# Routing tail of an RWKV, top-1 MoE and MLP kernel: tile 11's diagonal products earlier on ScalarE, and scalings, one-hots, slots and low rows of tiles 9 to 11 on GpSimd

## The chip, the cores and the metric

The kernel runs on one core of a Trainium2 chip. The metric is device time in microseconds (us) of one execution, taken as the median of several runs; one further execution was recorded by the hardware profiler. Engine names are those of the profile: PE is TensorE's matmul, PEld its weight load, DVE is VectorE, ACT is ScalarE, POOL is GpSimd, SP is the engine that issues most of the transfers. A q behind a name (SPq, POOLq) means the engine's instruction queue.

## The reference, cut to what matters

```python
def reference(**kwargs):
    attn_out = _attn_ref(...)          # linear attention: state = w*state + k v^T, y = r (state + u k v^T)
    x = attn_out.transpose(0, 2, 1, 3).reshape(1536, 384)
    x = _moe_ref(x, ...)
    return _moe2_ref(x, ...)           # h = x @ w_in; g = h * clip(h + 3, 0, 6) / 6; g @ w_out

def _moe_ref(x, w_gate, w1, w2, capacity):
    logits = x @ w_gate                # 8 experts
    expert_idx = argmax(logits)        # one expert for a token
    gate_w = softmax(logits)[expert_idx]
    for i in range(N):                 # tokens take the expert's places in order, up to capacity
        e = expert_idx[i]
        if counts[e] < capacity:
            disp[e, counts[e]] = x[i]; pos[i] = counts[e]; counts[e] += 1; keep[i] = True
    y = relu(disp @ w1) @ w2           # for each expert
    out[i] = gate_w[i] * y[expert_idx[i], pos[i]] if keep[i] else 0
```

## The kernel before

The kernel has three stages: attention with routing (to about 88 us in the trace), the experts (to about 219 us), and the last MLP. All of its instructions are placed by hand: each engine works through its own list in the order in which the code was written, and a semaphore holds an instruction until what it needs is there. An instruction that waits holds everything behind it on its engine.

Attention works on 12 tiles of 128 tokens, called T or t. For a tile, `bonus(T)` lets ACT write the diagonal products (8 small activations, one for each head, scaled by `dg`) into the tile x; `values` and `carried` are matmuls; `finish_x` adds their sum to x on DVE; `turn` transposes x on PE and ACT copies the result to `xT`; `gate` multiplies it with the gate's weights. Then comes `route(t)`: a list of about a dozen small DVE steps, handed out by `tick`. They find the largest logit, the one-hot of the chosen expert (`oh_all`), the ranks among tokens (`rank_mm`, a few small PE matmuls that `ranks` issues), the softmax scale `sm`, and `sf`, the token's place. `slots` is that place as an integer. Tiles 0 to 7 are routed in groups of four, whose scales are called `gsm`.

The rows of x, multiplied by the scale, go into the table `xs` in DRAM, sorted by expert, by one indirect transfer for each tile (`scale`, then `scatter`, L703; GpSimd issues it). `fetch(e)` reads an expert's first 224 rows back into `xr`. `fetch(0)` comes behind the scatters of tiles 0 to 8. Tiles 9, 10 and 11 reach expert 0 in another way, without the table: `first` is a one-hot of 128 tokens by 224 places, `lasth` the scaled rows rounded to the short format, `lastl` the remainder ("low rows"), and `late_rows(t)` multiplies both by the one-hot on PE into `px` (L684). The rows out of `xr` are added to `px` by transposing matmuls (L879). When `px` is whole, ACT and DVE cast it to `xh` and `xl` (L925 to L929), and the first expert matmul `psm` (L997) starts. Tiles 9 to 11 are scattered all the same, because the other experts need them. These three scatters write the table that `fetch(0)` reads, so the first of them waits until that read has landed.

Weights arrive in pieces of 768 KB, `raw`; ACT rounds a piece to its high part (`wah`, `wbh`) and DVE or GpSimd make the low part (`wal`, `wbl`, L188 and L194). `keep_warm(n)` issues n matmuls on zeros.

Of the kernel before, what the change touches and what calls it, by code (L numbers as in the profile page):

```python
# [8 lines left out]
F32 = mybir.dt.float32  # L9
# [11 lines left out]
P = 128  # L21
# [24 lines left out]
WIN = 224  # L46
# [19 lines left out]
def kernel(  # L66
# [150 lines left out]
        for _ in range(n):  # L217
            begin(lo_eng=lo_eng)

    late, px0, first, last_h, last_l = [], [], {}, {}, {}  # L220
    xr_t = {}
    spreads, places, outs = [], [], []

# [18 lines left out]
    def attention():  # L242
        actx = ExitStack()
        with actx:
# [343 lines left out]
            def route(t):  # L588
                if t < GRP * NGRP:
                    if t % GRP == GRP - 1:  # L590
                        route_group(t - GRP + 1)
                    return
                last, tail = t >= LATE, t == NTILE - 1
                pl = lgt.pop(t)
                l, po = pl[:, 0:E], pl[:, 64:64 + 2 * E]
                rk, pe = pl[:, 192:192 + E], pe_all[:, t, :]
                oh = oh_all[:, t, :]
                oh2 = oh.unsqueeze(1).to_broadcast([P, 2, E])
                slot = slots[:, t:t + 1]
# [12 lines left out]
                def rank_mm():  # L612
                    base_mm(po, t, True, False)
                    nc.tensor.matmul(po, tri, oh2, start=False, stop=True)

                def inverse():
                    V.reciprocal(sm, sm)
                    if last:
                        hi = lastp.tile([P, DM], F32R, name=f"lasth{t}")
                        nc.scalar.activation(hi, x_t[t], AF.Copy, scale=sm)  # L620
                        last_h[t] = hi
                        if t == NTILE - 2:
                            nc.scalar.activation(x_t[t], x_t[t], AF.Copy, scale=sm)
                            lo = lastp.tile([P, DM], F32R, name=f"lastl{t}")
                            nc.gpsimd.tensor_tensor(out=lo, in0=x_t[t], in1=hi.bitcast(F32), op=ALU.subtract)
                            last_l[t] = lo

                def low_rows():
                    o = first[t]
                    if t != NTILE - 2:  # L630
                        lo = lastp.tile([P, DM], F32R, name=f"lastl{t}")
                        V.scalar_tensor_tensor(
                            out=lo, in0=xs_t[t], scalar=sm, in1=last_h[t].bitcast(F32), op0=ALU.mult, op1=ALU.subtract
                        )
                    else:
                        lo = last_l[t]
                    first[t] = ((last_h[t], o), (lo, o))

                def done():
                    if last:  # L640
                        o = lastp.tile([P, WIN], F32R, name=f"first{t}")
                        V.tensor_scalar(
                            out=o, in0=col, scalar1=sf, scalar2=None, op0=ALU.is_equal
                        )
                        first[t] = o
                        xs_t[t] = x_t[t]
                        last_ops[t] = [low_rows]
                    V.tensor_scalar(out=slot, in0=sf, scalar1=float(FAR), scalar2=None, op0=ALU.add)
                    if t == NTILE - 2:
                        ready.append((slot, x_t.pop(t)))  # L650
                    else:
                        scat.append((slot, x_t.pop(t), sm))

                todo.append([
                    lambda: V.tensor_reduce(out=mx, in_=l, axis=AX.X, op=ALU.max),
                    lambda: V.scalar_tensor_tensor(
                        out=rk, in0=l, scalar=mx, in1=rank, op0=ALU.is_equal, op1=ALU.mult
                    ),
                    diff,
                    lambda: V.tensor_reduce(out=m2, in_=rk, axis=AX.X, op=ALU.max),  # L660
                    lambda: V.tensor_tensor(out=oh, in0=rk, in1=m2.to_broadcast([P, E]), op=ALU.is_equal),
                    [0, rank_mm],
                    lambda: V.tensor_reduce(out=sm, in_=gex[:, t % GRP, :], axis=AX.X, op=ALU.add),
                    inverse,
                    lambda: V.tensor_tensor(
                        out=sel, in0=po.rearrange("p (a e) -> p a e", a=2), in1=oh2, op=ALU.mult
                    ),
                    lambda: V.tensor_reduce(out=pe.unsqueeze(2), in_=sel, axis=AX.X, op=ALU.add),
                    lambda: V.tensor_scalar(
                        out=sf, in0=pe[:, 0:1], scalar1=cap_f, scalar2=pe[:, 1:2], op0=ALU.is_lt, op1=ALU.mult  # L670
                    ),
                    done,
                ])

# [72 lines left out]
            for T in range(NTILE - 1):  # L747
# [49 lines left out]
                    scatter()  # L797
                if T == 10:
                    drain(1)
                    scale()  # L800
                    scatter()
                    scatter()
                    scale()
# [29 lines left out]
            load_to(7)  # L833
            T = NTILE - 1
            carried(T)
            bonus(T)
            values(T, 0)
            ranks(0)
            keep_warm(3)
# [1 line left out]
            finish_x(T, 0)  # L841
            drain(0)
            values(T, 1)
            keep_warm(3)
            gate(T - 1)
            finish_x(T, 1)
            load_to(8)
            keep_warm(2, 0)
            route(T - 1)
            tick(3)  # L850
            turn(T)
            tick(2)
            finish(T - 2)
            late_rows(LATE, 0)
            keep_warm(2, 0)
            ranks(0)
            keep_warm(3, 0)
            tick(5)
            gate(T)
            route(T)  # L860
            xr = xr_t.pop(0)
            todo.reverse()
            tick(5)
            late_rows(LATE, 1)
            keep_warm(3, 0)
            ranks(0)
            todo.reverse()
            while len(todo) > 1:
                tick()
            finish(T - 1)  # L870
            tick(2)
            drain(0)
            finish(T)
            scale()
            scatter()
            keep_warm(3, 0)
# [6 lines left out]
            late_rows(LATE + 1)  # L883
            late_rows(T)
            scatter()
            scale(nc.vector)
            scatter()
            late.extend((lambda: rest(nc.vector, slice(HC, PC)), lambda: low(nc.vector)))

# [548 lines left out]
```

## Time and profile before

| what | us |
|---|---|
| median of 3 runs | 428.57 |
| lowest and highest | 428.19, 429.74 |
| the profiled execution's own time | 428.45 |
| its span, first to last instruction | 426.7 |
| PE, DVE, ACT, POOL busy in the span | 414.3, 256.2, 204.1, 177.0 |
| mean granted clock of TensorE | 0.995 |

The span is 1.75 us shorter than the profiled execution's own time; what lies around the span is start and end. PE is busy for 97% of the span, but a busy PE also counts matmuls that wait in its pipeline, so the order of events around the change has to be read from the timeline.

### The profile page before, as it was taken

How to read it: one execution, taken by the hardware profiler on the slowest of the kernel's cores; microseconds unless marked ns; L12 is line 12 of the kernel's file. 1: busy time of each engine (PE TensorE's matmuls, PEld its weight loads, DVE VectorE, ACT ScalarE, POOL GpSimd, SP SyncE). 2: the span in 40 equal slices, each digit the busy share in tenths (PEclk: the TensorE clock that was granted, in tenths of full speed). 3: DMA queues.
4: the chain of work that ended last, by engine and by line, in shares of the span. 5: the costliest groups of instructions: out<-in, count | busy, mean ns of one | idle time of the engine just before them, and what ended most of it. 6: DMA issues, size and time to landing. Idle time of an engine off the chain costs nothing.

```text
span 426.7 us, 8128 instructions
## 1 busy us (share of the span) xinstructions
PE 414.3 (97%) x3165; PEld 401.4 (94%) x3165; DVE 256.2 (60%) x474; ACT 204.1 (48%) x434; POOL 177.0 (41%) x146
## 2 busy tenths in 40 slices
PE   7999999999999999999999999999999999999992
PEld 4789999899999999999999999999999999999992
DVE  6997999797886775886978689661313022130310
ACT  2364569665735746757536263352505134260520
POOL 4875594327667567466000000002625225260441
PEclk9999999999999999999999999999999999999998
DMA  7988999556398898998521610001000000100001
GB/s 215 247 259 261 285 351 386 205 200 270 103 236 282 214 306 241 258 306 237 204 84 65 212 61 28 0 5 52 3 37 20 0 2 0 57 1 2 0 22 44
DMA packets 15953, 61.41 MB, mean 144 GB/s; under 512 B 2912, under 2 KB 4832, under 8 KB 15904
## 3 DMA queue, kind: packets, MB, share of 16 engines
q1 hardware_dynamic: 11808, 53.78, 40.9%
q0 software_dynamic: 1968, 4.73, 3.1%
q10 hardware_dynamic: 2128, 2.27, 1.8%
q8 instruction: 27, 0.44, 0.5%
q14 instruction: 22, 0.18, 0.1%
HBM read 53.30 MB, written 7.48 MB: 142 GB/s over the span
## 4 chain that ended last, share of the span: by engine, by line
PE 71%; DVE 8%; issue 8%; DMA 6%; POOL 4%; ACT 2%; SPq 0%; POOLq 0%; DVEq 0%; ACTq 0%
PE psh L1115 20%; PE pso L1138 20%; PE psm L997 11%; PE pym L1036 6%; DMA raw<-in_w_dram 4%; PE pym L1032 3%; PE py L421 2%; DMA hTt<-in_hT_dram 2%; POOL gl L1104 2%; PE pym L1033 2%; DVE A L400 1%; PE psa L394 1%; DVE rTt L354 1%; PE py L413 1%; PE pl L475 1%
## 5 line engine op out<-in xcount | busy, mean ns | idle before, releaser
L1119 DVE SCALAR_TENSOR_TENSOR g<-g,psh 128x384 f32<-128x384 f32 x64 | 35.4, 553 | 98.8 <-ACT g L1118 98.4
L1118 ACT ACTIVATE g<-psh,three 128x384 f32<-128x384 f32 x64 | 37.4, 584 | 73.3 <-PE psh L1115 73.2
L1104 POOL TENSOR_TENSOR gl<-g,gh 128x384 fp32r<-128x384 f32 x40 | 40.3, 1012 | 51.1 <-ACT gh L1103 51.1
L1156 POOL DMA_INDIRECT out_dram<-o,cid x12 | 11.8, 981 | 116.1 <-ACT o L1154 107.9
L1032 PE MATMUL pym<-h,wbh 128*128 128x448 f32 x120 | 38.4, 378 | 0.1
L194 POOL TENSOR_TENSOR wal<-raw,wah 128x1536 fp32r<-128x1536 f32 x7 | 24.6, 3519 | 24.0 <-ACT wah L188 15.9
L1103 ACT CAST gh<-g 128x384 fp32r<-128x384 f32 x64 | 32.3, 504 | 3.5 <-DVE g L1119 3.5
L1003 ACT ACTIVATE h<-psm 128x448 fp32r<-128x448 f32 x32 | 17.5, 548 | 31.1 <-PE psm L997 29.0
L1115 PE MATMUL psh<-y2l,wbh 128*128 128x384 f32 x96 | 32.4, 337 | 0.0
L1115 PE MATMUL psh<-y2l,wah 128*128 128x384 f32 x96 | 32.4, 337 | 0.0
L1115 PE MATMUL psh<-y2h,wah 128*128 128x384 f32 x96 | 32.3, 336 | 0.0
L1115 PE MATMUL psh<-y2h,wbh 128*128 128x384 f32 x96 | 32.3, 336 | 0.0
L1115 PE MATMUL psh<-y2h,wbl 128*128 128x384 f32 x96 | 32.1, 335 | 0.0
L1115 PE MATMUL psh<-y2h,wal 128*128 128x384 f32 x96 | 32.1, 335 | 0.0
L1138 PE MATMUL pso<-wah,gh 128*128 128x384 f32 x96 | 32.1, 334 | 0.0
L1138 PE MATMUL pso<-wbh,gh 128*128 128x384 f32 x96 | 32.1, 334 | 0.0
L1138 PE MATMUL pso<-wbh,gl 128*128 128x384 f32 x96 | 32.1, 334 | 0.0
L1138 PE MATMUL pso<-wal,gh 128*128 128x384 f32 x96 | 32.1, 334 | 0.0
L1138 PE MATMUL pso<-wah,gl 128*128 128x384 f32 x96 | 32.1, 334 | 0.0
L1138 PE MATMUL pso<-wbl,gh 128*128 128x384 f32 x96 | 32.1, 334 | 0.0
L997 PE MATMUL psm<-xh,wah 128*128 128x224 f32 x192 | 31.9, 275 | 0.1
L997 PE MATMUL psm<-xh,wal 128*128 128x224 f32 x192 | 31.7, 275 | 0.0
(192 smaller groups left out, 1144.0 us busy)
## 6 DMA issues: line engine op xcount, KB each, us to landing
raw<-in_w_dram SPq DMA_DIRECT2D x32, 768.0 KB, 7.9
tokt<-in_tok_dram SPq DMA_DIRECT2D x12, 576.0 KB, 6.2
raw<-in_w_in_dram SPq DMA_DIRECT2D x8, 768.0 KB, 4.8
raw<-in_w_out_dram SPq DMA_DIRECT2D x8, 768.0 KB, 5.0
hTt<-in_hT_dram SPq DMA_DIRECT2D x12, 448.0 KB, 7.3
xs<-zero SPq DMA_DIRECT2D x8, 336.0 KB, 5.3
xr<-xs ACTq DMA_DIRECT2D x6, 336.0 KB, 7.3
xr<-xs SPq DMA_DIRECT2D x2, 336.0 KB, 3.5
```

The source lines that it names most:

```text
L194: eng.tensor_tensor(out=lo[:, sl][:, h], in0=raw[:, h], in1=hi[:, sl][:, h].bitcast(F32), op=ALU.subtract)
L997: nc.tensor.matmul(ps[:, fi, :], wa_tile(a, k, 2 * q + fi), b[:, k, :], start=n == k == 0 and not (both and fi), stop=n == 2 and k == KD - ...
L1003: nc.scalar.activation(hh, ps, AF.Relu)
L1032: nc.tensor.matmul(py[k], w2h[:, w], h2, start=f == 0, stop=False)
L1036: nc.tensor.matmul(py[k // 2][:, k % 2, :], a[:, w], h2[:, i], start=n == 0, stop=n == 3 * NF - 1)
L1103: nc.scalar.copy(gh, g)
L1104: (nc.vector if any(do) else nc.gpsimd).tensor_tensor(out=gl, in0=g, in1=gh.bitcast(F32), op=ALU.subtract)
L1115: nc.tensor.matmul(ps, wa_tile(a, k, f), y, start=n == 0, stop=n == 3 * KD - 1)
L1118: nc.scalar.activation(g, ps, AF.Relu, bias=three)
L1119: nc.vector.scalar_tensor_tensor(out=g, in0=g, scalar=6.0, in1=ps, op0=ALU.min, op1=ALU.mult)
L1138: nc.tensor.matmul(po, a[:, sl], c[:, wo], start=(h == 0 or (b, s) in acc) and f == 0 and n == 0, stop=(h == 1 or defer) and f == NF - 1 a ...
L1156: apart(outs, nc.gpsimd.indirect_dma_start(out=out, out_offset=bass.IndirectOffsetOnAxis(ap=cid[:, t:t + 1], axis=0), in_=o, in_offset=Non ...
```

## The change

ACT's order in iteration T = 10 changes: `bonus(11)` stands ahead of a weight cast of 1536 columns and ahead of one scaling, and the scaling of tile 7 goes to GpSimd. For tiles 9 and 10 the one-hots `first`, the `slots` and the low rows go from DVE to GpSimd; their scaling is on ACT for both. For tile 11 these stay on DVE, and its scaling goes from DVE to GpSimd. The tail's order is written anew: `gate(11)` stands ahead of tile 9's rows, tile 9's scatter ahead of tile 10's one-hot, and the transposes of `xr` behind tile 10's rows. Eight of 19 keep-warm matmuls are gone.

```diff
-                        if t == NTILE - 2:
+                        if not tail:
                             nc.scalar.activation(x_t[t], x_t[t], AF.Copy, scale=sm)
...
+                    if tail:
                         V.scalar_tensor_tensor(
                             out=lo, in0=xs_t[t], scalar=sm, in1=last_h[t].bitcast(F32), op0=ALU.mult, op1=ALU.subtract
                         )
                     else:
-                        lo = last_l[t]
+                        nc.gpsimd.tensor_tensor(out=lo, in0=xs_t[t], in1=last_h[t].bitcast(F32), op=ALU.subtract)
...
+                own = nc.gpsimd if last and not tail else V
+
+                def spots():
+                    o = lastp.tile([P, WIN], F32R, name=f"first{t}")
+                    own.tensor_scalar(
+                        out=o, in0=col, scalar1=sf, scalar2=None, op0=ALU.is_equal
+                    )
...
+                    own.tensor_scalar(out=slot, in0=sf, scalar1=float(FAR), scalar2=None, op0=ALU.add)
+                    if last and not tail:
                         ready.append((slot, x_t.pop(t)))
...
                 if T == 10:
                     drain(1)
-                    scale()
+                    bonus(T + 1)
+                    scale(nc.gpsimd)
                     scatter()
                     scatter()
                     scale()
...
             carried(T)
-            bonus(T)
             values(T, 0)
...
+            gate(T)
+            finish(T - 2)
+            scatter()
+            late_rows(LATE)
+            tick(7)
+            finish(T - 1)
+            scatter()
+            route(T)
             tick(5)
             keep_warm(3, 0)
             ranks(0)
+            late_rows(LATE + 1)
+            tick(6)
+            finish(T)
             drain(0)
+            xr = xr_t.pop(0)
             for n in range(2 * KD):
                 k, c = divmod(n, 2)
                 nc.tensor.matmul(
                     px0[k][:, c * HW:(c + 1) * HW], xr[:HW, c, k * P:(k + 1) * P], ident[:HW, :HW],
...
             late_rows(T)
-            scatter()
-            scale(nc.vector)
+            scale(nc.gpsimd)
             scatter()
```

In the order lists below, `x_757`, `x_834`, `x_917`, `x_1022` and `x_1124` are the tiles x of t = 6, 7, 8, 9 and 10; `x_1255` is that of t = 11 before, and `x_1218` that of t = 11 now. The bracket names the semaphores that an instruction waits for: `DMAHW` those of transfers issued by SP or ACT, `DMASW` those of GpSimd's indirect transfers.

On ACT, in iteration T = 10, this stands before:

```order
L693 ACTIVATE x_757<-x_757,gsm_985 128x384
L693 ACTIVATE x_834<-x_834,gsm_985 128x384
L693 ACTIVATE x_917<-x_917,sm_1098 128x384 [waits DVE_49]
L610 ACTIVATE gex_239<-d_1194 128x8 [waits DVE_49]
L188 CAST wah_1015<-raw_913 128x1536 [waits DMAHW5_49]
L429 ACTIVATE x_1255<-tokt_832,dg_1200 128x48 [waits DMAHW4_49,DMASW2_49]
L429 ACTIVATE x_1255<-tokt_832,dg_1200 128x48 x7
L466 COPY xT_1280<-pt_1276 128x384 [waits PE_49,Activation_49]
```

And this now:

```order
L694 ACTIVATE x_757<-x_757,gsm_985 128x384
L429 ACTIVATE x_1218<-tokt_832,dg_1200 128x48 [waits DMAHW4_49,DMASW2_49,DVE_49]
L429 ACTIVATE x_1218<-tokt_832,dg_1200 128x48 x7
L694 ACTIVATE x_917<-x_917,sm_1098 128x384 [waits DVE_49]
L610 ACTIVATE gex_239<-d_1194 128x8 [waits DVE_49]
L188 CAST wah_1015<-raw_913 128x1536 [waits DMAHW5_49]
L466 COPY xT_1280<-pt_1276 128x384 [waits PE_49,Activation_49]
```

The eight products of tile 11 moved ahead of the cast, and the scaling of tile 7 left ACT.

On GpSimd, from the scatter of tile 6 to the end of the tail, this stands before (tile 10's low rows, then the scatters of tiles 10, 9 and 11):

```order
L703 DMA xs_60<-x_757,slots_76 12288x384 [waits Activation_49]
L703 DMA xs_60<-x_834,slots_76 12288x384 [waits Activation_49]
L703 DMA xs_60<-x_917,slots_76 12288x384 [waits DMASW0_49,DVE_49,Activation_49]
L625 TENSOR_TENSOR lastl10_1354<-x_1124,lasth10_1351 128x384 [waits DVE_49,Activation_49]
L703 DMA xs_60<-x_1124,slots_76 12288x384 [waits DMAHW2_49,DMASW1_49,DVE_49]
L703 DMA xs_60<-x_1022,slots_76 12288x384 [waits DMASW2_49,Activation_49]
L703 DMA xs_60<-x_1255,slots_76 12288x384 [waits DMASW3_49,DVE_49]
```

Now the scaling of tile 7 (`L696 TENSOR_SCALAR x_834<-x_834,gsm_985 128x384`) stands ahead of the scatter of tile 6, and from the scatter of tile 8 on the engine has:

```order
L704 DMA xs_60<-x_917,slots_76 12288x384 [waits DMASW0_49,DVE_49,Activation_49]
L640 TENSOR_SCALAR first9_1291<-col_250,sf_1198 128x224 [waits DVE_49]
L648 TENSOR_SCALAR slots_76<-sf_1198 128x1
L633 TENSOR_TENSOR lastl9_1339<-x_1022,lasth9_1285 128x384 [waits Activation_49]
L704 DMA xs_60<-x_1022,slots_76 12288x384 [waits DMAHW2_49,DMASW1_49,Pool_49]
L640 TENSOR_SCALAR first10_1361<-col_250,sf_1314 128x224 [waits DVE_49]
L648 TENSOR_SCALAR slots_76<-sf_1314 128x1
L633 TENSOR_TENSOR lastl10_1364<-x_1124,lasth10_1355 128x384 [waits Activation_49]
L704 DMA xs_60<-x_1124,slots_76 12288x384 [waits DMASW2_49,Pool_49]
L696 TENSOR_SCALAR x_1218<-x_1218,sm_1372 128x384 [waits DVE_49,PE_49]
L704 DMA xs_60<-x_1218,slots_76 12288x384 [waits DMASW3_49,DVE_49,Pool_49]
```

The first late scatter, which waits for the landing of `fetch(0)` (`DMAHW2_49`), stood behind tile 10's low rows; now tile 10's one-hot, slots and low rows stand behind it.

On PE, from the rank matmul of tile 11 to the first expert matmul, the list now is this (before, the six transposes of `xr` stood ahead of tile 10's rows):

```order
L614 MATMUL pl_1335<-oh_all_65,tri_230 128x16
L685 MATMUL px_1344<-first10_1361,lasth10_1355 128x224 [waits Activation_49,Pool_49]
L685 MATMUL px_1344<-first10_1361,lastl10_1364 128x224 [waits Pool_49]
L873 MATMUL px_1344<-ident_63,xr_1250 128x112 [waits DMAHW2_49]
L685 MATMUL px_1344<-first11_1404,lasth11_1399 128x224 [waits DVE_49,Activation_49]
L685 MATMUL px_1344<-first11_1404,lastl11_1406 128x224 [waits DVE_49]
L989 MATMUL psm_1464<-xh_1438,wah_1015 128x224 [waits Activation_49]
```

Of the three parts of `px` only the first stands here. Tile 10's two products wait for GpSimd where the earlier list waited for DVE; the cast of `px` on ACT (`L917 CAST xh_1438<-px_1344`) now also waits for GpSimd's scaling of tile 11, whose memory it reuses.

## Rows read from the trace of the kernel before

**Rows 1.** The page's first line.

```profile
span 426.7 us, 8128 instructions
```

**Rows 2.** The chain that ended last, 83 to 92 us: start, us, what.

```profile
84.36 0.27 PE pl L512 x5
...
85.16 1.33 PE px L879 x12
86.49 0.92 PE px L684 x8
...
87.56 0.35 ACT xh L925
...
87.96 4.15 PE psm L997 x34
```

**Rows 3.** Timeline of ACT, 73 to 79.5 us: start, us, instructions.

```profile
75.83 1.46 ACT L188 CAST wah<-raw 128x1536 fp32r<-128x1536 f32 x1
77.19 1.91 ACT L429 ACTIVATE x<-tokt,dg 128x48 f32<-128x48 f32 x8
79.01 0.46 ACT L466 COPY xT<-pt 128x384 f32<-128x384 f32 x1
```

**Rows 4.** Timeline of DVE, 62 to 92 us: in brackets the idle time before, and its releaser.

```profile
78.91 0.36 DVE L435 TENSOR_TENSOR x<-py,x 128x192 f32<-128x192 f32 x1 [1.56 <-ACT x L429]
```

**Rows 5.** Timeline of PE, 66 to 92 us.

```profile
78.35 1.03 PE L421 MATMUL py<-tokt,A 128*128 128x96 f32 x8
...
79.22 0.65 PE L258 MATMUL psw<-zero 128*128 128x384 bf16 x3
79.70 0.73 PE L475 MATMUL pl<-wg_sb,xT 128*128 128x8 f32 x6
...
80.87 0.55 PE L464 MATMUL pt<-ident,x 128*128 128x128 f32 x3
...
82.63 0.73 PE L475 MATMUL pl<-wg_sb,xT 128*128 128x8 f32 x6
```

**Rows 6.** Timeline of POOL, 74 to 90 us.

```profile
73.53 0.97 POOL L703 DMA_INDIRECT xs<-x,slots  x1 [0.30 <-ACT xT L466]
...
77.36 0.98 POOL L703 DMA_INDIRECT xs<-x,slots  x1 [0.30 <-DVE wal L194]
83.81 0.99 POOL L625 TENSOR_TENSOR lastl<-x,lasth 128x384 fp32r<-128x384 f32 x1 [5.47 <-ACT x L623]
```

**Rows 7.** SP's timeline; then the landing of the scatter at 77.36, and of `fetch(0)`.

```profile
80.07 0.34 SPq L236 DMA_DIRECT2D xr<-xs  x1
...
DMA to landing us min/median/max: 2.7/2.7/2.7
...
DMA to landing us min/median/max: 3.3/3.3/3.3
```

**Rows 8.** POOL's groups by form, 0 to 92 us: busy us, mean ns, then idle before.

```profile
L376 POOL TENSOR_TENSOR ktt<-tokt,Tet 128x384 f32<-128x384 f32 x9 | 9.5, 1051 | 10.0 <-DMA tokt<-in_tok_dram 4.8 <-PE pu L442 3.1 <-PE psa L394 2.0
L742 POOL IOTA col<- 128x224 f32 x1 | 0.3, 310 | 0.0
L713 POOL TENSOR_SCALAR_AFFINE_SELECT am<-am 128x128 f32<-128x128 f32 x1 | 0.3, 292 | 0.1
L727 POOL IOTA rank<- 128x8 f32 x1 | 0.1, 143 | 0.0
```

**Rows 9.** The chain that ended last, 90 to 150 us.

```profile
129.15 1.90 DVE wal L194
...
131.12 8.37 DMA raw<-in_w_dram
```

**Rows 10.** Windows at the end: PE, PEld, DVE, ACT, POOL busy, granted clock, DMA.

```profile
418.00:420.00 2.00, 0.80 (x5) 0.48 (x3) 0.00 (x0) 0.49 (x1) 0.35 (x1) 1.00 0.03 6
...
422.00:424.00 2.00, 0.00 (x0) 0.00 (x0) 0.00 (x0) 0.00 (x0) 0.00 (x0) 0.66 0.05 14
```

**Rows 11.** Timeline of PE, 0 to 26 us: its longest idle time before 83 us.

```profile
8.95 0.71 PE L394 MATMUL psa<-rTt,kd 48*128 48x128 f32 x8 [1.01 <-DVE rTt L325]
```

More of the change, by code (lines that the diff above doesn't have):

```diff
@@ L218, in turn_over @@
             begin(lo_eng=lo_eng)
-    late, px0, first, last_h, last_l = [], [], {}, {}, {}
+    late, px0, first, last_h = [], [], {}, {}
     xr_t = {}
@@ L621, in inverse @@
                         last_h[t] = hi
-                        if t == NTILE - 2:
+                        if not tail:
                             nc.scalar.activation(x_t[t], x_t[t], AF.Copy, scale=sm)
-                            lo = lastp.tile([P, DM], F32R, name=f"lastl{t}")
-                            nc.gpsimd.tensor_tensor(out=lo, in0=x_t[t], in1=hi.bitcast(F32), op=ALU.subtract)
-                            last_l[t] = lo
                 def low_rows():
                     o = first[t]
-                    if t != NTILE - 2:
-                        lo = lastp.tile([P, DM], F32R, name=f"lastl{t}")
+                    lo = lastp.tile([P, DM], F32R, name=f"lastl{t}")
+                    if tail:
                         V.scalar_tensor_tensor(
@@ L635, in low_rows @@
                     else:
-                        lo = last_l[t]
+                        nc.gpsimd.tensor_tensor(out=lo, in0=xs_t[t], in1=last_h[t].bitcast(F32), op=ALU.subtract)
                     first[t] = ((last_h[t], o), (lo, o))
-                def done():
[L640 to L649, printed above, removed]
+                own = nc.gpsimd if last and not tail else V
[4 more added lines that the diff above has]
+                    )
+                    first[t] = o
+                    xs_t[t] = x_t[t]
+                    last_ops[t] = [low_rows]
+                def done():
+                    own.tensor_scalar(out=slot, in0=sf, scalar1=float(FAR), scalar2=None, op0=ALU.add)
+                    if last and not tail:
                         ready.append((slot, x_t.pop(t)))
@@ L671, in route @@
                     ),
+                    *([spots] if last else []),
                     done,
@@ L843, in attention @@
             values(T, 1)
-            keep_warm(3)
             gate(T - 1)
@@ L847, in attention @@
             load_to(8)
-            keep_warm(2, 0)
+            keep_warm(3, 0)
             route(T - 1)
@@ L852, in attention @@
             tick(2)
-            finish(T - 2)
-            late_rows(LATE, 0)
             keep_warm(2, 0)
             ranks(0)
-            keep_warm(3, 0)
-            tick(5)
[L859 to L864, printed above, removed]
+            gate(T)
[6 more added lines that the diff above has]
+            route(T)
+            tick(5)
             keep_warm(3, 0)
             ranks(0)
[L867 to L871, printed above, removed]
+            late_rows(LATE + 1)
+            tick(6)
+            finish(T)
             drain(0)
-            finish(T)
-            scale()
-            scatter()
-            keep_warm(3, 0)
+            xr = xr_t.pop(0)
             for n in range(2 * KD):
@@ L882, in attention @@
                 )
-            late_rows(LATE + 1)
             late_rows(T)
-            scatter()
-            scale(nc.vector)
+            scale(nc.gpsimd)
             scatter()
```

## The prediction

> **What bounds the kernel now.** I read the chain of waits first, back from the end of the program. From 88 us on it is almost all matmul, so what the tail of the routing costs is the moment at which the first expert matmul starts: 87.96 us of a span of 426.7 [rows 1, 2]. Before that moment the chain goes from the DVE steps of tile 11's routing over its rank matmul (84.36) and a packed PE (the transposes of `xr` from 85.16, the rows of tiles 10 and 11 from 86.49) to the cast of `px` at 87.56. The reader is to see that DVE's last low rows and PE's list arrive there within a few tenths of each other.
>
> Then I read each engine's timeline for what sets these moments. On ACT the weight cast at 75.83 stands ahead of tile 11's products at 77.19 [rows 3], and DVE idles 1.56 us for these [rows 4]. On PE the gate of tile 10 starts at 79.70, the transposes of tile 11 at 80.87, the gate of tile 11 at 82.63 [rows 5]. On GpSimd the scatters stand 1.28 us apart, the last of the early ones starts at 77.36, and then the engine idles 5.47 us [rows 6]. That scatter lands 2.7 us after its start, which releases `fetch(0)` at 80.07, and this lands 3.3 us later, at 83.37 [rows 7].
>
> **The change, part by part.** First what comes earlier. Tile 11's products no longer stand behind the cast, so they end by about 76 us, before the matmul sums they are added to. DVE's wait of 1.56 us goes. What is late next is PE: the second half of these sums runs from 78.35 for 1.03 us, to 79.38 [rows 5]. Without the three keep-warm matmuls in between, the gate of tile 10 follows at 79.22, where these started, rather than at 79.70 (0.16 us each). One more of them now stands behind it, so the transposes of tile 11 come at about 80.3 rather than 80.87. In the new order the gate of tile 11 has no rows and no keep-warm matmuls of its own ahead: transposes 0.55 [rows 5], copy to `xT` 0.46 [rows 3], so it starts at about 81.35 instead of 82.63. From 82.63 to the rank matmul of tile 11 at 84.36 it took 1.73 us [rows 2, 5]; that is now 83.1. Tiles 9's and 10's one-hots, slots and the low rows of tile 9 leave DVE as well, so it has tile 11's low rows ready by about 85. ACT's one added scaling (tile 9's) and the missing keep-warm matmuls lie in time that nothing waits for. On these engines alone the expert stage would start about 1.3 us earlier.
>
> Second, what comes later, and all of it is on GpSimd. The scaling of tile 7 stands ahead of three scatters, and no row shows a scaling or a one-hot on this engine. The bounds: IOTA writes without reading, 143 ns for 8 columns and 310 for 224, so 0.77 ns a column: 0.43 us for a scaling of 384 columns and 0.31 for a one-hot of 224. TENSOR_TENSOR reads two operands, 1.05 us for 384, so 0.61 for 224 [rows 8]. In between is AFFINE_SELECT, which reads one operand and writes one, as the new instructions do: 292 ns for 128, with IOTA's 143 as the start 1.24 ns a column. That gives 0.61 for the scaling and 0.41 for the one-hot, and I take 0.60 and 0.41; slots are one column, 0.14 at most. Of this the Trainium skill, GPSIMD Engine Reference, section 4.1 (Engine selection), says that elementwise work belongs on VectorE and that GpSimd is about twice as slow for two-input operations but roughly at line rate for one-input ones. By it, half of the two-input row is an estimate for both, 0.5 and 0.3, and the sum below would be 0.2 us smaller; no row here shows it.
>
> The chain on GpSimd then is this. The scatter of tile 8 starts 0.60 later, so `fetch(0)` lands at 83.37 + 0.60 = 83.97. Tile 9's scatter waits for that landing, since it writes the table that the fetch reads. The same wait was in the program before, but behind tile 10's low rows, where nothing of expert 0 stood behind it. Now tile 10's one-hot, slots and low rows stand behind it, and PE waits for them. Start 0.30 after the release, as between any two of these transfers [rows 6]: 84.27. Its 0.98 us: 85.25. One-hot 85.66, slots 85.80, low rows 0.99 [rows 6]: 86.79. PE still has to do then what it did from 85.16 to the cast at 87.56, less the three products with tile 10's high rows: 2.40 - 3 x 0.92 / 8 = 2.05 us [rows 2]. With 0.04 for the semaphore the cast comes at 88.88 and the first expert matmul 0.40 later, at 89.28, which is 1.32 us later than 87.96.
>
> The cast also waits for GpSimd's scaling of tile 11, behind the scatter of tile 10: 86.79 + 0.30 + 0.98 + 0.60 = 88.67, just earlier than PE. With the lower prices (0.43, 0.31) the start is 1.05 us later than before. With the upper ones (1.05, 0.61) low rows come at 87.44, the scaling of tile 11 ends at 89.77 and decides: 90.21, or 2.25 later.
>
> Behind the start the shift goes through one to one. The first weight transfer on the chain behind that start, 8.37 us from 131.12, is issued when DVE has made a low part at 129.15, which stands in DVE's list behind the expert's own work [rows 9]. The second fetch, for expert 1, follows the scatter of tile 11, which starts at about 89.0 instead of 88.11, less late than PE itself.
>
> Sum: the profiled execution took 428.45 us, its span 426.7; 428.45 + 1.32 = 429.77. The median of the runs shown is 428.57, 0.12 above that execution, so I put the new median at 429.9. About 0.5% (2.1 us) is what a measurement of this kernel can tell from no change, and 1.3 us is 0.3%.
>
> **Rivals.** *The clock falls* (this ends on the other side: slower). PE would be idle from the rank matmul at about 83.4 to tile 10's one-hot at 85.66, 2.3 us, and again for most of the time to 86.79. Before, the longest idle time in the attention stage was 1.01 us, and the clock stayed at full [rows 11]. At the end of the program PE has nothing to do from 418.8 on, and in the window from 422 the granted clock is 0.66, full for 0.64 us and then at the half level, 1.2 GHz: it fell when PE had been idle for some 3.8 us [rows 10]. An idle time like the new one is in no row, so neither answer is excluded. It decides if the granted clock is below full between 86.8 and 89: if PE's 2.05 us between tile 10's low rows and the cast run at half rate, they take 2.05 more, and the time is 431.9. The Trainium skill, TensorE: Matmul & The Clock Gate, Part 1, says that the clock is at half rate after idling and at full rate after sustained work. The half level at the end agrees.
>
> *The wait does not hold.* If the fetch had landed by 81.2, when tile 9's low rows are done, tile 10's low rows would be ready near 84.1, the expert stage would start at about 86.5, and the time would be 1.4 us less than before, 427.1. For it speaks all of the first part; against it the landing at 83.37, which would have to come 2.8 us earlier than I work out although its scatter starts later.
>
> *Made up later.* If the weight transfers set the pace of the experts by themselves, a later start would cost nothing, and the time would be 428.6. A transfer on the chain [rows 9] speaks for it. Against it speaks that this transfer waits for a buffer that the experts' own work frees.
>
> **How the numbers follow.** I give the forecast 0.68, the clock 0.13, the wait that does not hold 0.06, made up later 0.13. The likeliest case alone reaches from 429.2 to 431.0 (its bounds 1.05 and 2.25, and some tenths for landings, which differ from transfer to transfer). The range takes in the case of no change below and most of the way to the clock's above: 428.3 to 431.7. Slower by over 0.5% begins at 430.7: the clock's 0.13 and 0.04 of the forecast's upper end, 0.17. Faster by over 0.5% would be under 426.4, which no case reaches; 0.02 for what I don't see. The rest, 0.81, is within 0.5%.
>
> **What would show it.** Right: GpSimd idle after tile 9's low rows until about 84, then tile 9's scatter and tile 10's one-hot behind it; PE idle between tile 11's rank matmul and tile 10's rows; gate of tile 11 near 81.4; first expert matmul near 89.3; GpSimd's scaling near 0.6 us. Wrong: tile 9's scatter starts before 83, or the first expert matmul is no later than 88, or the granted clock is below 1.00 between 84 and 95, or the time at which the last MLP starts shifts by another amount than the first expert matmul.

## The result, and the profile after

The changed kernel took 433.97 us (median of 6 runs, 431.96 to 436.64) against 430.03 us for the kernel before (median of 6 runs): a ratio of 1.0104, with a 95% interval of 1.0056 to 1.0153. It is slower by about 4.5 us by this ratio, and by 3.9 us by the two medians; 429.9 was forecast, with a range up to 431.7. Medians here and below are over all runs, the ratios leave out a few long ones at a lower clock, and so a ratio is not the quotient of two medians. The profiled execution took 434.51 us, which is 6.06 us more than that of before; the two traces thus lie further apart than the runs do, since that of before (428.45) was a short one. The page's first lines and its line on PE now read:

```profile
span 432.7 us, 8109 instructions
...
PE 416.7 (96%) x3157; PEld 404.1 (93%) x3157; DVE 252.2 (58%) x468; ACT 203.6 (47%) x433; POOL 183.4 (42%) x153
```

PE is still busy nearly all of the span, so the answer lies again in the stretch before the first expert matmul. On GpSimd the timeline of the changed kernel shows (to be held against [rows 6, 8]):

```profile
74.83 1.29 POOL L696 TENSOR_SCALAR x<-x,gsm 128x384 f32<-128x384 f32 x1
...
77.62 1.65 POOL L704 DMA_INDIRECT xs<-x,slots  x1 [0.30 <-issue]
79.58 0.98 POOL L704 DMA_INDIRECT xs<-x,slots  x1 [0.30 <-ACT xT L466]
80.59 0.87 POOL L640 TENSOR_SCALAR first<-col,sf 128x224 fp32r<-128x224 f32 x1
81.43 0.23 POOL L648 TENSOR_SCALAR slots<-sf 128x1 int32<-128x1 f32 x1
81.62 0.99 POOL L633 TENSOR_TENSOR lastl<-x,lasth 128x384 fp32r<-128x384 f32 x1
85.97 1.07 POOL L704 DMA_INDIRECT xs<-x,slots  x1 [3.36 <-DMA xr<-xs]
87.08 0.88 POOL L640 TENSOR_SCALAR first<-col,sf 128x224 fp32r<-128x224 f32 x1
87.92 0.23 POOL L648 TENSOR_SCALAR slots<-sf 128x1 int32<-128x1 f32 x1
88.11 0.99 POOL L633 TENSOR_TENSOR lastl<-x,lasth 128x384 fp32r<-128x384 f32 x1
...
90.39 1.27 POOL L696 TENSOR_SCALAR x<-x,sm 128x384 f32<-128x384 f32 x1
```

The reader is to see three things: a scaling costs 1.28 us and a one-hot 0.87 here; the scatter at 85.97 waited 3.36 us for the read of expert 0 (`DMA xr<-xs`); and tile 10's one-hot, slots and low rows stand behind it. Of the low rows only tile 9's are new on GpSimd: tile 10's were made there before as well, at 83.81 [rows 6]. The read is issued by SP at 82.18 [rows 7]:

```profile
82.18 0.34 SPq L236 DMA_DIRECT2D xr<-xs  x1
```

PE's timeline in the changed kernel (against [rows 2, 5]):

```profile
81.83 0.83 PE L475 MATMUL pl<-wg_sb,xT 128*128 128x8 f32 x6
...
83.90 0.17 PE L614 MATMUL pl<-oh_all,tri 128*128 128x16 bf16 x1
88.01 0.98 PE L685 MATMUL px<-first,lasth 128*128 128x224 f32 x3 [3.94 <-POOL first L640]
89.15 0.98 PE L685 MATMUL px<-first,lastl 128*128 128x224 f32 x3 [0.16 <-POOL lastl L633]
89.93 2.76 PE L873 MATMUL px<-ident,xr 112*128 112x112 f32 x12
...
93.77 1.34 PE L989 MATMUL psm<-xh,wah 128*128 128x224 f32 x6
```

PE waits 3.94 us for tile 10's one-hot, and then works slowly: the transposes of `xr` take 2.76 us. The windows (columns as in [rows 10]) say why. The granted clock is full from 24 us until shortly after 87 us, falls while PE idles, is 0.50 to about 94, and full again:

```profile
84.00:86.00 2.00, 0.07 (x3) 0.00 (x0) 1.55 (x6) 0.61 (x1) 0.03 (x1) 1.00 0.71 223
86.00:88.00 2.00, 0.00 (x0) 0.00 (x0) 0.00 (x0) 0.00 (x0) 1.95 (x3) 0.82 1.05 384
88.00:90.00 2.00, 1.83 (x7) 1.56 (x8) 0.00 (x0) 0.00 (x0) 1.82 (x3) 0.50 0.72 264
...
92.00:94.00 2.00, 2.00 (x11) 1.92 (x9) 0.36 (x2) 0.35 (x1) 0.96 (x1) 0.50 0.25 93
94.00:96.00 2.00, 2.00 (x16) 1.78 (x16) 2.00 (x6) 1.99 (x3) 0.00 (x0) 0.97 0.16 30
```

In this trace the clock had been at 0.50 once before, from about 15.6 to 22.4 us, which it had not in the trace of before.

So the first expert matmul comes at 93.77 instead of 87.96, 5.81 us later. The last MLP's first matmul on the chain starts at 225.16 us, against 219.01 before, 6.15 later (the first of these lines is from before, the second from now):

```profile
219.01 12.49 PE psh L1115 x72
...
225.16 12.49 PE psh L1107 x72
```

What the routing's tail lost was not made up afterwards.

### The profile page after: what moved, and what is told of

Same layout as the page of the kernel before. It is cut to its first block, busy times and chain, and to the rows that moved or that the text cites. A ratio compares the mean times of both kernels' runs of the same rounds, so it can differ in the third digit from the quotient of the medians.

```text
span 432.7 us, 8109 instructions
## 1 busy us (share of the span) xinstructions
PE 416.7 (96%) x3157; PEld 404.1 (93%) x3157; DVE 252.2 (58%) x468; ACT 203.6 (47%) x433; POOL 183.4 (42%) x153
## 4 chain that ended last, share of the span: by engine, by line
PE 63%; issue 5%; POOL 2%; DVE 1%; POOLq 0%; DVEq 0%
PE psh L1107 20%; PE pso L1130 19%; PE psm L989 11%; PE pym L1024 6%; PE pym L1028 3%; PE pym L1025 3%; POOL gl L1096 2%; PE px L907 1%; POOL out_dram L1148 1%; DVE wal L194 1%; DVE h L996 0%; DVE y2h L1065 0%; POOLq L1358 0%; DVE y2l L1066 0%; POOLq L1096 0%
## 5 line engine op out<-in xcount | busy, mean ns | idle before, releaser
L989 PE MATMUL psm<-xl,wah 128*128 128x224 f32 x192 | 31.7, 275 | 0.0
```

The source lines that it names most:

```text
L989: nc.tensor.matmul(ps[:, fi, :], wa_tile(a, k, 2 * q + fi), b[:, k, :], start=n == k == 0 and not (both and fi), stop=n == 2 and k == KD - ...
```

## The experiments

The theory after the result: three things add up. GpSimd's prices are about twice those assumed; tile 9's scatter holds tile 10's work until the read of expert 0 has landed; and PE's idle time, which follows from both, halves the clock. The rivals: the prices alone, the wait alone, or the clock alone. Since executions differ by up to 1.9 us already before this place, the traces are compared by one stretch, from the start of tile 11's `carried` matmuls (L413) to the first expert matmul. It starts here (the first line is from before, the second from the changed kernel):

```profile
75.40 1.14 PE L413 MATMUL py<-z,rTt 48*128 48x96 f32 x16
...
75.86 1.14 PE L413 MATMUL py<-z,rTt 48*128 48x96 f32 x16
```

"Change" is that stretch against before's 12.56 us, from one trace of each kernel; the ratio is over several runs. "The order" stands for the place of tile 9's scatter, ahead of tile 10's work on GpSimd. The kernels are numbered in the order in which they are told.

| kernel | L413 | first `psm` | stretch | change | ratio, 95% interval |
|---|---|---|---|---|---|
| before | 75.40 | 87.96 | 12.56 | | 1 |
| changed | 75.86 | 93.77 | 17.91 | +5.35 | 1.0104, 1.0056 to 1.0153 |
| 1 scatter behind | 75.62 | 89.76 | 14.14 | +1.58 | 1.0053, 1.0012 to 1.0094 |
| 2 and tile 11's scaling on DVE | 74.78 | 86.41 | 11.63 | -0.93 | 1.0006, 0.9968 to 1.0043 |
| 3 keep-warm | 75.47 | 91.55 | 16.08 | +3.52 | 1.0082, 1.0044 to 1.0120 |
| 4 tile 7's scaling on ACT | 75.05 | 92.53 | 17.48 | +4.92 | 1.0125, 1.0049 to 1.0201 |
| 5 one-hots on DVE | 74.09 | 90.89 | 16.80 | +4.24 | 1.0104, 1.0067 to 1.0141 |
| 6 neither the order nor the prices | 75.09 | 86.19 | 11.10 | -1.46 | 0.9962, 0.9940 to 0.9983 |
| 7 the earlier products and tile 7's scaling | 74.90 | 87.86 | 12.96 | +0.40 | 1.0022, 0.9998 to 1.0046 |
| 8 the order alone | 76.14 | 91.53 | 15.39 | +2.83 | 1.0051, 1.0023 to 1.0079 |
| 9 the order alone, kept warm | 77.26 | 91.32 | 14.06 | +1.50 | 1.0023, 0.9997 to 1.0050 |

**1. The wait taken away.** Tile 9's scatter stands behind tile 10's low rows, as it did before.

```diff
             finish(T - 2)
-            scatter()
             late_rows(LATE)
             tick(7)
             finish(T - 1)
+            scatter()
             scatter()
```

> The changed kernel with one move: tile 9's scatter stands behind tile 10's one-hot, slots and low rows on GpSimd. Theory A, the queue (tile 9's scatter waits for the fetch and holds tile 10's rows, PE idles, the clock falls): tile 10's low rows end near 85 instead of 89.1, PE's 3.9 us of idle time goes, but the cast of px still waits for the scaling of tile 11, now behind two scatters: first expert matmul near 89.5 to 90, time about 4 us under the changed kernel, some 1.5 to 2 above the kernel before. The clock stays full unless PE's new idle time of about 2.3 us ahead of the cast is enough for it. Theory B, the prices (GpSimd's slow scalings and one-hots are late wherever the scatter stands): first expert matmul within 1 us of 93.8, time unchanged.

Measured: 430.64 us, against 427.32 for before, so still slower by about 2.3 us (ratio 1.0053). Tile 10's low rows are ready at 84.32 instead of 89.10, and PE has multiplied all rows by 87.2. Now the cast of `px` waits, for GpSimd's scaling of tile 11 (88.03 to 89.32). The timelines of PE and GpSimd in this run:

```profile
85.65 1.08 POOL L704 DMA_INDIRECT xs<-x,slots  x1 [1.33 <-DMA xr<-xs]
87.04 0.99 POOL L704 DMA_INDIRECT xs<-x,slots  x1 [0.30 <-issue]
88.03 1.29 POOL L696 TENSOR_SCALAR x<-x,sm 128x384 f32<-128x384 f32 x1
...
89.76 1.62 PE L989 MATMUL psm<-xh,wah 128*128 128x224 f32 x6 [2.59 <-ACT xh L917]
```

The first expert matmul is 3.77 us nearer to `carried` than in the changed kernel, so the scatter's place brings most of the loss ahead of the experts, and theory B is wrong. But PE idles 2.59 us for the cast, and its windows show the clock falling in that idle time:

```profile
88.00:90.00 2.00, 0.24 (x1) 0.24 (x2) 0.64 (x2) 0.64 (x3) 1.71 (x3) 0.87 0.72 257
90.00:92.00 2.00, 2.00 (x10) 2.00 (x11) 2.00 (x5) 2.00 (x2) 0.62 (x1) 0.50 0.51 197
...
94.00:96.00 2.00, 2.00 (x11) 2.00 (x11) 1.45 (x2) 0.52 (x1) 0.00 (x0) 0.50 1.01 328
96.00:98.00 2.00, 2.00 (x22) 1.98 (x22) 1.08 (x2) 0.54 (x1) 0.00 (x0) 0.92 1.00 396
```

Here the slow stretch lies in the experts' own work: from the first expert matmul to the last MLP it is 133.91 us instead of before's 130.89. Together with the +1.58 that is 4.6 us in this trace; at 433.46 us it is one of the longer executions of this kernel.

**2. That scaling back on DVE as well.** The edit of 1, and:

```diff
-            scale(nc.gpsimd)
+            scale(nc.vector)
```

(in the tail, for tile 11).

> As the run before, and the scaling of tile 11 is on DVE again, so that nothing on the way to px waits for a transfer. Theory A: the first expert matmul starts between 87 and 88 at the full clock, and the time is that of the kernel before, from 1.0 less to 0.3 more. Theory B: about 2 us or more above the kernel before.

Measured: 428.42 us against 427.32. In its trace the clock is 1.00 in every window from 82 to 98, PE's transposes of `xr` start at 84.02, straight behind tile 10's rows, the first expert matmul comes at 86.41 (87 to 88 was expected), and the profiled execution is 427.0 us. The runs do not show that gain, and do not exclude it: 0.93 us would be a ratio of 0.998, which lies in the interval. What follows for certain is that in 1 it was this scaling that the cast waited for.

**3. Only the clock held up.** The changed kernel with 24 keep-warm matmuls in PE's idle time.

```diff
             ranks(0)
+            keep_warm(24, 0)
             late_rows(LATE + 1)
```

> The changed kernel with 24 more keep-warm matmuls (3.9 us) between tile 11's rank matmul and tile 10's rows, so that PE is not idle; nothing else moves. If the low clock is a part of the loss: the granted clock stays at full until the expert stage, PE's work from tile 10's low rows to the first expert matmul takes 2.5 us instead of 4.6, the first expert matmul starts near 91.7, where GpSimd's scaling of tile 11 ends, and the time is 2.0 to 2.5 us under the changed kernel. If the wait alone is the loss: no change.

Measured: 431.42 us against 427.32. PE's timeline in this run:

```profile
83.61 4.06 PE L258 MATMUL psw<-zero 128*128 128x384 bf16 x24
87.46 0.60 PE L685 MATMUL px<-first,lasth 128*128 128x224 f32 x3
88.61 0.59 PE L685 MATMUL px<-first,lastl 128*128 128x224 f32 x3 [0.55 <-POOL lastl L633]
89.04 1.50 PE L874 MATMUL px<-ident,xr 112*128 112x112 f32 x12
```

And the window in which the changed kernel had 0.50:

```profile
88.00:90.00 2.00, 1.45 (x13) 1.40 (x13) 0.00 (x0) 0.00 (x0) 1.78 (x3) 1.00 0.49 187
```

The clock stays at 1.00 in every window, the transposes of `xr` take 1.50 us instead of 2.76, and the stretch is 1.83 us shorter than in the changed kernel. The runs show the same of the clock: its mean over an execution is 0.988 to 0.997 in all ten, against 0.979 to 0.986 in the six of the changed kernel. In the time they do not tell the two apart, since the ratios' intervals overlap. The rest, 3.52 us over before, stays: the clock is a part of the loss, not all of it. After the rows it is again GpSimd's scaling of tile 11 (it ends at 91.12) that the cast waits for.

**4. Tile 7's scaling back on ACT.**

```diff
                     bonus(T + 1)
-                    scale(nc.gpsimd)
+                    scale()
                     scatter()
```

> The changed kernel with one part undone: tile 7's scaling is on ACT, behind tile 11's products, not on GpSimd. Theory A: GpSimd's 1.29 us ahead of three scatters go, the fetch lands 0.7 to 1.3 us earlier (ACT's scaling of tile 8 comes 0.5 later), and so do tile 9's scatter and the first expert matmul; PE's idle time is 2.6 to 3.2 us instead of 3.9. Time 0.7 to 1.3 us under the changed kernel if the clock still falls, about 3 under it if not. Theory B, that the one-hots alone are the price: the same 0.7 to 1.3, and no idle time on GpSimd ahead of tile 9's scatter.

Measured: 434.11 us against 427.32, the interval too wide to tell it from the changed kernel. The 1.29 us on GpSimd are gone, but the scatter of tile 7 now waits 1.06 us for ACT, since the products of tile 11 stand ahead of the scaling there. The stretch shrinks by 0.43 us only, where both theories had at least 0.7. GpSimd still idles 3.46 us ahead of tile 9's scatter, so theory B is wrong; PE still idles 3.63 us and the clock falls.

**5. The one-hots and slots of tiles 9 and 10 back on DVE**, in the changed kernel.

```diff
-                own = nc.gpsimd if last and not tail else V
+                own = V
```

> The changed kernel, but tiles 9's and 10's one-hots and slots stay on DVE; tile 9's scatter still stands ahead of tile 10's low rows on GpSimd. Theory (the one-hot, 0.88 us, and the slots, 0.23 us, stand on the path behind the scatter, but the scatter's wait and the clock are the larger part): tile 10's low rows start straight behind the scatter, some 1.1 us earlier than in the changed kernel, near 87.0; tile 10's one-hot is on DVE long before, so PE has high rows to multiply earlier and then idles for about 3 us at most; the granted clock still falls to 0.50 as it did in the run with the scatter behind (2.6 us of idle time), the first expert matmul comes near 92 and the time is 432 to 433. Rival 1 (only the one-hots' price on GpSimd matters): the time falls to 428 to 429. Rival 2 (PE's idle time is broken up by the high rows, and the clock stays at 1.00): first expert matmul near 90, time near 430.5.

Measured: 432.42 us against 427.54; the stretch is 1.11 us shorter than in the changed kernel, as much as the 0.88 and 0.23 us that left GpSimd's chain. The ratio is the same as the changed kernel's; its interval would not show 1.1 us. The high rows did come earlier and PE still idled 3.54 us behind them. The clock fell in that idle time (0.86 between 84 and 86 us, 0.50 after it), so rival 2 is wrong, and at this time rival 1 too.

**6. Neither the order nor the prices.** The edits of 2 and 5, and tile 7's scaling on DVE. Of the change this keeps the earlier products, tile 9's low rows on GpSimd and, but for tile 9's scatter, the new order of the tail.

```diff
                     bonus(T + 1)
-                    scale(nc.gpsimd)
+                    scale(nc.vector)
                     scatter()
```

> The run with the scatter behind and tile 11's scaling on DVE, and besides this the scaling of tile 7 on DVE and tiles 9's and 10's one-hots and slots on DVE: of the change only the earlier products, the low rows of tile 9 on GpSimd and the new order of the tail remain. Theory (all that was put on GpSimd costs, the rest of the change gains): the last early scatter starts 1.3 us earlier than in the changed kernel, the first expert matmul comes at 86.0 to 86.4 (before 87.96; 86.41 in the run with tile 11's scaling on DVE), the clock stays at 1.00, and the profiled execution is 1.4 to 1.8 us shorter than that of before, a ratio of 0.996 to 0.997. Rival (the early start is given back later): the expert matmul comes as early, but the last MLP starts within 0.3 us of before's 219.01.

Measured: 426.32 us against 427.54, a ratio of 0.9962. This is the one version that the runs show faster than both kernels. Its chain:

```profile
83.30 0.77 PE px L685 x6
84.06 1.33 PE px L873 x12
...
85.80 0.35 ACT xh L917
...
86.19 4.37 PE psm L989 x36
```

DVE's timeline has tile 7's scaling:

```profile
74.74 0.41 DVE L696 TENSOR_SCALAR x<-x,gsm 128x384 f32<-128x384 f32 x1
```

PE works almost without a gap, and the clock stays at 1.00 in every window from 76 to 100. The eight keep-warm matmuls are missing here too, so their absence alone does not bring the clock down. The same scaling that took GpSimd 1.28 us takes DVE 0.41. The last MLP starts 2.07 us earlier than before, so the rival is wrong.

**7. The earlier products and tile 7's scaling.** The kernel before, with two of the change's edits.

```diff
                 if T == 10:
                     drain(1)
-                    scale()
+                    bonus(T + 1)
+                    scale(nc.gpsimd)
...
             carried(T)
-            bonus(T)
             values(T, 0)
```

> The kernel before, with one part of the change alone: tile 11's products ahead of the cast, and tile 7's scaling on GpSimd. Theory (the scaling's price on GpSimd matters only where a fetch is waited for, and before, nothing of expert 0 stood behind the scatter of tile 9): the scaling takes 1.3 us, the read of expert 0 starts 1.3 us later than 80.07 and lands near 84.7, DVE's wait of 1.56 us for the products is gone, and the first expert matmul comes within 0.5 us of 87.96; the time is that of before within 0.3%. Rival 1 (the later read delays PE's transposes, which started at 85.16): first expert matmul 0.5 to 1.3 us later, time 428.9 to 429.7. Rival 2 (the earlier products alone give the gain): first expert matmul 0.5 to 1.5 us earlier.

Measured: 428.64 us against 427.54, a ratio of 1.0022 whose interval takes in 1. In its profiled execution the clock fell at about 66.6 us, far ahead of the edit and not inside an idle time: PE had been idle for 0.99 us and then busy again for 1.9.

```profile
64.67 1.30 PE L413 MATMUL py<-z,rTt 48*128 48x96 f32 x16 [0.99 <-DVE x L435]
...
66.00:68.00 2.00, 2.00 (x18) 1.99 (x18) 1.97 (x6) 2.00 (x9) 0.85 (x1) 0.65 1.02 422
```

So a further execution was recorded:

> The same kernel as the run of the first part alone, for a trace of an execution in which the clock did not fall in attention. Expected as there: the scaling of tile 7 takes 1.3 us on GpSimd, the read of expert 0 starts near 81.4, the first expert matmul comes within 0.5 us of 87.96.

It shows, on GpSimd, SP and PE:

```profile
74.68 1.29 POOL L695 TENSOR_SCALAR x<-x,gsm 128x384 f32<-128x384 f32 x1
...
81.41 0.34 SPq L236 DMA_DIRECT2D xr<-xs  x1
...
84.81 1.59 PE L879 MATMUL px<-ident,xr 112*128 112x112 f32 x12 [0.46 <-DMA xr<-xs]
```

DVE's 1.56 us for the products [rows 4] are gone. The read of expert 0 is 1.34 us later, as expected, and just late enough that PE waits 0.46 us for it. The first expert matmul is within 0.1 us of before's, in an execution that was 0.5 us earlier at `carried`. Together the two edits give nothing while the old order of PE's list stands; what the earlier products would give without the later read was not run. The price on GpSimd is nearly hidden there.

**8. The order alone.** The kernel of 6, with tile 9's scatter put ahead of tile 10's low rows again.

```diff
             finish(T - 2)
+            scatter()
             late_rows(LATE)
             tick(7)
             finish(T - 1)
-            scatter()
             scatter()
```

> The faster run of before (all that was put on GpSimd back on DVE, except low rows), but tile 9's scatter stands ahead of tile 10's low rows again, as in the changed kernel: the order of that wait alone, at none of the prices. Theory (the order is enough by itself: PE idles, and the clock falls): the read of expert 0 starts near 79.9 and lands near 83.2, tile 9's scatter starts at 83.5 to 84.2, tile 10's low rows are ready near 85.6, PE idles about 3 us before them, the granted clock falls to 0.50 some time from 85 on and stays there for 5 to 7 us, the first expert matmul comes at 88.5 to 90.5, and the time is 1.5 to 3.5 us above that of before, a ratio of 1.003 to 1.008. Rival (the prices on GpSimd brought the fall of the clock, and without them it stays at 1.00): first expert matmul near 88.4, ratio 0.999 to 1.002.

Measured: 430.61 us against 428.52. In its profiled execution too the clock fell long before, at about 67.4 us and 1.4 us after an idle time of 0.99 had ended, so the trace is of a further one:

> The same kernel as the run of the order alone, for a trace of an execution in which the clock did not fall in attention. Expected as there: tile 10's low rows ready near 85.6, PE idle about 3 us before them, then either the granted clock at 0.50 for some us and the first expert matmul at 88.5 to 90.5, or the clock at 1.00 and the first expert matmul near 88.4.

The timelines of SP, GpSimd and PE there:

```profile
80.86 0.34 SPq L236 DMA_DIRECT2D xr<-xs  x1
...
84.83 0.99 POOL L704 DMA_INDIRECT xs<-x,slots  x1 [2.78 <-DVE pe_all L668]
85.85 1.01 POOL L633 TENSOR_TENSOR lastl<-x,lasth 128x384 fp32r<-128x384 f32 x1
...
86.91 0.98 PE L685 MATMUL px<-first,lastl 128*128 128x224 f32 x3 [2.13 <-POOL lastl L633]
```

And the window in which PE waits:

```profile
86.00:88.00 2.00, 1.09 (x5) 1.09 (x6) 1.99 (x4) 0.00 (x0) 1.83 (x2) 0.69 0.95 336
```

For the scatter the profile names DVE's `pe_all`, the event that came last. But the scatter waits for the read's landing, earlier scatters and its own slots, and DVE had made these slots by 80.1: it was the read, which landed 3.2 us after its issue. With none of GpSimd's dear prices the scatter still starts 3.97 us after that issue, PE idles 2.13 us (about 3 was expected), and the clock falls. The first expert matmul comes at 91.53, a us behind the expected range; 0.74 of that is this execution's late `carried`, where its clock had also been at 0.50 from 15 to 22 us. The rival is wrong: the order is enough by itself, and the intervals of 8 and 6 lie apart.

**9. The order alone, kept warm.** The kernel of 8 with `keep_warm(16, 0)` ahead of tile 10's rows, where 3 had 24.

> The order alone, with 16 keep-warm matmuls ahead of tile 10's rows. Theory (about half of what the order costs is the clock's): the clock stays at 1.00, the first expert matmul comes at 88.2 to 88.8, within 0.5 us of where the start of tile 10's low rows puts it, and the ratio is 0.999 to 1.003, below the 1.0051 of the order alone. Rival (the order costs by its wait, the clock nothing more): the ratio stays at 1.004 to 1.006.

Measured: 428.60 us against 427.59. The clock is 1.00 in every window from 80 to 100, also where PE idled in 8:

```profile
86.00:88.00 2.00, 2.00 (x15) 1.25 (x13) 1.97 (x5) 0.08 (x1) 1.48 (x2) 1.00 1.00 381
```

The stretch is 1.33 us shorter than in 8, and 2.96 us longer than in 6. So what remains is the wait; the intervals of 9 and 6 lie apart, so the runs show it too. The ratio lies where the theory has it, but the intervals of 8 and 9 overlap, so the clock's part is shown by the traces alone. The first expert matmul comes at 91.32, not near 88.5. This execution was late already at `carried`, by 1.86 us (its clock had been at 0.50 from about 15 to 21 us); without that it is 89.46, still behind the expected range; the read was issued 0.46 us later behind `carried` than in 8.

## Why the prediction was wrong, point by point

The order of events was read rightly: the wait on GpSimd, and PE idle behind it. Two steps failed. GpSimd's instructions were priced too low, and PE's work behind the wait stands in the sum at the full clock, where it ran at half rate; that rival had got 0.13 and is what happened.

**What comes earlier** was right. The gate of tile 11 came at 81.83, with `carried` 0.46 us late in this execution: 81.37 against the forecast of 81.35. DVE had tile 11's low rows at about 85.8 (by about 85 was forecast), which nothing waited for. "About 1.3 us earlier" on these engines alone is what run 6 gives, 1.46 in the stretch.

**GpSimd's prices: this step failed.** 0.60 us was assumed for a scaling, 0.41 for a one-hot, "0.14 at most" for slots; measured are 1.28, 0.87 and 0.23. The first two are above even the upper bound, 1.05 and 0.61, which came from a row with two operands. DVE idled during tile 10's one-hot and tile 11's scaling, so the prices are not due to DVE working at the same time. The row that was nearest was no bound: AFFINE_SELECT and IOTA [rows 8] are other instructions, and this one, on one operand and a scalar for each partition, costs more for 384 columns than TENSOR_TENSOR does (0.99). On the chain to the first expert matmul that is 0.68 for the scaling (1.28 less 0.60), and 0.48 for tile 10's one-hot and slots: these two start 1.03 us before the low rows, where 0.55 was assumed. 1.16 us in all. The Trainium skill, GPSIMD Engine Reference, section 4.1 (Engine selection), calls one-input work on this engine roughly line rate; the trace doesn't agree, 1.28 us stands beside DVE's 0.41, and by that rule the sum would have been further off still.

**The wait behind the read** held as forecast: GpSimd idle from 82.6, then the scatter, then tile 10's one-hot. One of its terms was too low. The scatter is worked out to start 3.60 us after the read's issue, 3.30 for the landing and 0.30 from there; it took 3.79 here, and 3.79 to 4.16 in all eight traces in which a scatter waits for this read (changed, 1 to 5, 8, 9). Where the landing is on record it came 3.0 to 3.4 us after the issue, and the scatter started about 0.75 behind it. The 0.30 came from transfers that followed one another without such a wait. Together with an early scatter that took 1.65 us instead of 0.98, and tile 9's that held GpSimd for 1.11, this part came 0.69 us later than worked out. "The wait does not hold" is refuted.

**The clock: the chance was wrong.** The prediction set the new idle time (2.3 us) beside the only fall that a row showed, at some 3.8 us of idle time at the end [rows 10], and gave the fall 0.13. The idle time became 3.94, since prices and wait were longer. But an idle time like the forecast one would have been enough as well: in runs 1 and 8 the clock fell inside idle times of 2.59 and 2.13 us. It did so in each of the five traces with an idle time of 2.13 us or more in the tail (changed, 1, 4, 5, 8), while the tails of before, 2, 3, 6, 7 and 9, which had none, kept the full clock. The Trainium skill, TensorE: Matmul & The Clock Gate, Part 1, has the half rate after idling; these tails agree, and the granted clock of 0.50 is its lower level, 1.2 GHz. That a shorter idle time is safe is not shown. 1.01 us [rows 11] and 0.46 (run 7) left the clock full, but elsewhere it fell although PE had had no longer idle time than that since its first matmul: 1.9 and 1.4 us after 0.99 in the first traces of 7 and 8, and at 15.6 us in the changed kernel. Why, stays open. The price of 2.05 was about right: from the low rows at 89.10 to the first expert matmul it took 4.67 us, where 2.49 was worked out at the full clock. Of these 2.18 us, 0.50 is not the clock's: GpSimd's scaling of tile 11 ended at 91.66, and with the 0.43 from there to the first matmul (as in run 3) the start would have been 92.09 anyway. That leaves 1.68. Run 3 gave 1.83 back in the stretch, 1.67 of it behind the low rows; between 8 and 9 it is 1.89 there (4.67 and 2.78).

**The sum.** Forecast 89.28, measured 93.77. The 4.49 us between are 0.46 (this execution was late at `carried`), 0.69 (wait and transfers), 1.16 (prices on the way to the low rows), and 2.18 behind them (scaling of tile 11 0.50, clock 1.68). The runs give sizes from the other side, one step after the other: from before to run 6 -1.46, the wait +2.96 (run 9), the clock +1.33 (run 8), the two scalings +1.41 (run 5), one-hots and slots +1.11. That they add up to +5.35 is no test, since each step starts where the last ended. These are single traces, so each may be off by some tenths: 0.56 of run 9's wait are later transfers, and without these the wait is 2.40 and the clock 1.89.

**Behind the start**, "one to one" was right in the two traces: +5.81 at the first expert matmul, +6.15 at the last MLP, +6.06 in the whole execution. "Made up later" is refuted.

What stays open: how much of the gain in run 2's trace and of the difference between runs 3, 4, 5 and the changed kernel is there over many runs, since the intervals are as wide as these differences. That the wait costs at least what the rest of the change gains is shown by runs and traces; the sizes of the prices and of the clock's part are those of single traces.

## What to carry to other kernels

Before work moves to an engine with idle time, look at what stands in its queue: an instruction there that waits for a transfer holds everything placed behind it, and here that wait alone cost more than the whole change could give. An idle time that a change opens on PE is to be counted with the clock that may fall in it, as it did in each idle time of 2.13 us or more in these tails, and filling it (24 matmuls on zeros gave 1.83 us back in the trace) is second best to not opening it. For an instruction that no row shows, a row of another form may be no bound: on GpSimd the form with a scalar for each partition was dearer than the form with two tiles. A single instruction of it placed where it is nearly hidden, as in run 7, measures it at little cost.

## What had not been expected of the hardware

GpSimd's TENSOR_SCALAR took 0.23 us for one column, 0.87 for 224 and 1.28 for 384, which is about three times DVE's 0.41 for the last; TENSOR_TENSOR on 384 columns took 0.99 on the same engine. And the clock, once it had fallen, was at 0.50 in all windows from 88 to 94 us in the changed kernel and from 90 to 96 in run 1, although PE was busy again for most of both. It also fell in executions in which PE had not been idle for more than about 1 us since its first matmul.
